# Splitting weight loads, and one batch's v, into row-sized pieces

## The chip, the cores and the metric

The kernel runs on one core of a Trainium2 chip. The metric is the device time of one execution in microseconds (us); lower is better. Before the change the median of five runs is 1142.55 us (1142.17 to 1143.49).

A core has a matrix engine (TensorE, PE in the profile), a vector engine (DVE), a scalar engine (ACT), GpSimd (POOL) and SyncE (SP). Each runs its own program in order. SP, ACT and POOL also issue DMAs, which 16 DMA engines carry out.

## The reference

```python
def _attn_ref(u, v, z):                    # u, v: (8, 3008, 256), z: (8, 3008, 64)
    scores = (1 / S) * np.matmul(z, z.transpose(0, 2, 1))
    attn = np.maximum(scores, 0.0) ** 2
    return u * np.matmul(attn, v)

def _moe_ref(x, w_tok1, w_tok2, w_ch1, w_ch2):   # x is the result of _attn_ref
    xt = x.transpose(0, 2, 1)
    h = np.maximum(xt @ w_tok1, 0.0) @ w_tok2    # (3008, 256), (256, 3008)
    u = x + h.transpose(0, 2, 1)
    h2 = np.maximum(u @ w_ch1, 0.0) @ w_ch2      # (256, 1536), (1536, 256)
    return u + h2
```

All inputs and the output are float32.

## The kernel before

The eight batches are worked through one after the other. For each batch the 3008 positions are cut into six blocks of 512 (the last has 448). For a block q of queries and a group g of 512 keys, PE forms scores from zT, the transposed z (line 428, tile `sc`). ACT takes the relu into a bf16 tile `at` (line 466), DVE squares it (line 474), and PE multiplies it with v into an accumulator (line 657, tile `acc`). After six groups the accumulator is evacuated (ACT copies one half, line 783, DVE adds the other, line 789) and DVE multiplies it with uT, the transposed u (line 810, called the gate here), into `xT`. The scores are symmetric, so from batch 1 on a tile `at` of block (q, g) is also turned by a DMA transpose into `fl` (line 526, called a flip here), which serves as block (g, q). There are six `at` buffers (`ROOM["at"]`); a new `at` may be written only when the PE reads and the flip of the tile six before it are done. In batch 0 every block but the last is computed directly.

When a batch's six blocks are done, the mixer follows for this batch: PE multiplies with w_tok1 (line 864) and w_tok2 (line 883), then with w_ch1 (line 924) and w_ch2 (line 993). The mixer of one batch is interleaved with the attention of the next. The weights are loaded once, during the attention of batch 0, and stay in memory.

The order on every engine is fixed when the program is made: a planner in the kernel keeps the time at which each engine will be free and appends the work that can start soonest. Its costs are constants (a load counts as `LOAD = 1.3` us); they aren't touched by the change.

Loads of v, u, z (from batch 1 on) and of the weights are issued by POOL and cast from float32 to bf16 on the way. They are due at given groups of batch 0, which the function `at_group` collects: the six groups of batch 1's v, six loads each of w_tok1 and w_tok2, two of w_ch1 and two of w_ch2 are spread over batch 0, between the loads of u and of batch 1's z. POOL's loads take eight completion semaphores in turn, so that a load waits until the one eight before it has landed. SP issues all transposes: uT from u (line 230), x_sb from xT (line 824), zT from z (lines 138 and 142), the flips (lines 518 and 526).

`rows_of` lets partition p take n consecutive rows of a group, so that its part of a load is one contiguous run:

```python
    def rows_of(ap, c):
        n = full_tiles[c]
        return ap[c * QW:c * QW + n * P, :].rearrange("(p t) d -> p t d", t=n)
```

QW is 512, P is 128; n is 4 for the first five groups and 3 for the last one, whose 64 remaining rows are loaded by themselves (line 211 for v, line 242 for w_tok1). In bf16 a row of 256 values has 512 bytes.

Of the kernel before, what the change touches and what calls it, by code (L numbers as in the profile page):

```python
# [13 lines left out]
P = 128  # L14
QW = 512
GK = 4
# [40 lines left out]
def kernel(  # L57
# [11 lines left out]
    nc = tc.nc  # L69
    B, S, D = u.shape  # L70
# [12 lines left out]
    widths = [min(QW, S - q * QW) for q in range(NQ)]  # L83
# [13 lines left out]
    w_tok1_sb = consts.tile([P, KT, d_tok], BF16)  # L97
    w_tok2_sb = consts.tile([P, DT, S], BF16)
    w_ch1_sb = consts.tile([P, DT, d_ch], BF16)
# [11 lines left out]
# [5 lines that stand above are left out]
    def last_rows(ap):  # L116
        return ap[(KT - 1) * P:, :]
# [81 lines left out]
    def load_v(b, c):  # L199
        if b == 0:  # L200

            vt = sb.tile([P, GK, D], BF16, tag="fl", name="v_sb", bufs=ROOM["fl"])
            live["fl"] += 1
            fl_free.pop(0)
        else:
            vt = sb.tile([P, GK, D], BF16, tag="v", name="v_sb", bufs=8)
        n = full_tiles[c]
        nc.gpsimd.dma_start(out=vt[:, :n, :], in_=rows_of(v[b], c))
        if n < GK:
            for r in range(2):  # L210
                nc.gpsimd.dma_start(
                    out=vt[r * TAIL:(r + 1) * TAIL, n, :], in_=last_rows(v[b]))
        vs[b, c] = vt
        v_in[b, c] = Done(pe[0] + 9.0 if b > 1 else 0.0)
        loading(LOAD)
# [19 lines left out]

    def load_w_tok1(c):
        n = full_tiles[c]
        nc.gpsimd.dma_start(
            out=w_tok1_sb[:, c * GK:c * GK + n, :], in_=rows_of(moe_w_tok1, c))
        if n < GK:  # L240
            nc.gpsimd.memset(w_tok1_sb[TAIL:, KT - 1, :], 0.0)
            nc.gpsimd.dma_start(
                out=w_tok1_sb[:TAIL, KT - 1, :], in_=last_rows(moe_w_tok1))
        loading(LOAD)

    def load_w_tok2(c):
        cols = slice(c * QW, c * QW + widths[c])
        nc.gpsimd.dma_start(
            out=w_tok2_sb[:, :, cols],
            in_=moe_w_tok2.rearrange("(tc t) s -> t tc s", t=P)[:, :, cols])  # L250
        loading(LOAD)

    def load_w_ch(part):
        if part < 2:
            nc.gpsimd.dma_start(
                out=w_ch1_sb[:, part, :], in_=moe_w_ch1[part * P:(part + 1) * P, :])
        else:
            h = CHT // 2
            c0 = (part - 2) * h
            nc.gpsimd.dma_start(  # L260
                out=w_ch2_sb[:, c0:c0 + h, :],
                in_=moe_w_ch2.rearrange("(cc c) d -> c cc d", c=P)[:, c0:c0 + h, :])
        loading(LOAD * 1.5)
# [42 lines left out]
    def loading(us):  # L306
        loads[0] = max(loads[0], pe[0] + 1.0) + us
# [91 lines left out]
    def can_score(first_unit, most):  # L399

        n, at = 0, live["at"]
        for (b, q, g), pr in units[first_unit:first_unit + most]:
            if (b, q) not in turned or (b, g) not in turned:
                break
            at += pr == 0
            if at > ROOM["at"]:
                break
            n += 1
        return n
# [717 lines left out]
    make_identity(nc, ident)  # L1127
    zf0 = [first_z(c) for c in range(NG)]
    load_v(0, 0)
    nc.gpsimd.memset(zs[:, 0, :], 0.0)  # L1130
    nc.gpsimd.memset(zs[:, KT + 1, :], 0.0)

    after(zf0[NG - 2][:, 0, :1])
    for c in range(1, NG):
        load_v(0, c)
# [52 lines left out]
    def when_used(b, c, j):  # L1188
        ask(lambda: load_v(b + 1, c),
            lambda: j < 2 or used.get((b, vorder[j - 2]), 0) == NQ)  # L1190
# [85 lines left out]
    def ask_w_ch(part):  # L1276
        load_w_ch(part)
        w_done[part].t = pe[0] + 16.0
# [4 lines left out]
    def ask_w_tok2(c):  # L1283
        load_w_tok2(c)
        tok2_done[c].t = pe[0] + 10.0

    items = [lambda c=c: load_v(1, c) for c in vorder]
    items += [lambda c=c: load_w_tok1(c) for c in range(NG)]
    items += [lambda c=c: ask_w_tok2(c) for c in range(NG)]
    items += [lambda part=part: ask_w_ch(part) for part in range(4)]  # L1290
# [30 lines left out]
    while cur[0] is not None or heads or tails:  # L1321
        run_engines(pe[0])
        ask_some()
        t = pe[0]
# [15 lines left out]
        n = can_score(done_units, most)  # L1340
# [118 lines left out]
```

## Time and profile before

| | us |
|---|---|
| median of five runs | 1142.55 |
| the profiled execution, its time | 1142.55 |
| its span (first to last instruction) | 1140.8 |
| PE busy | 1133.7 |
| DVE busy | 642.0 |
| ACT busy | 548.7 |
| POOL busy | 147.0 |

The span is the stretch from the first instruction to the last; what lies around it is start and end of the execution. In the profile, "busy" is the time in which an engine has an instruction under way. The DMA share is the sum of the time of all DMA packets over the time of 16 engines; it can be above 1 since packets overlap. The queue q0 holds the loads that POOL issues, q1 the transposes and stores that SP issues. In a row of the timeline the columns are the start, the duration, the engine (SPq is SP's queue), the line, the operation and the tiles it writes and reads; x4 means that four such instructions were merged into one row. A stage row gives the stretch, its length, then for each engine the busy time and the number of instructions, the granted TensorE clock as a share of full speed, the DMA share and the rate.

The rows of loads show minimum, median and maximum of the time that POOL takes to issue one. Landing times are counted from the start of the issue to the completion semaphore.

### The profile page before, as it was taken

The page shows a single profiled execution, that of the slowest core. Times are in us where ns is not written, and L with a number is a line of the kernel's source. Part 1 is how long each engine was busy: PE and PEld are TensorE (multiplying, and loading weights), DVE is VectorE, ACT ScalarE, POOL GpSimd, SP SyncE. Part 2 cuts the span into 40 slices and gives each one's busy share as a digit, 9 for nine tenths or more (in the row PEclk, how much of TensorE's full clock was granted, in tenths as well). Part 3 has the DMA queues.
Part 4 walks back from the last instruction along what each step waited for, and adds up shares of the span by engine and source line. Part 5 has one row for each costly group of instructions (what it writes and reads, how often), then busy time and mean ns, then how long its engine had stood idle before and what let it go on. Part 6 is the DMA issues. An engine that isn't in the chain of part 4 may idle for free.

```text
span 1140.8 us, 22492 instructions
## 1 busy us (share of the span) xinstructions
PE 1133.7 (99%) x9219; PEld 678.1 (59%) x9219; DVE 642.0 (56%) x953; ACT 548.7 (48%) x702; POOL 147.0 (13%) x387
## 2 busy tenths in 40 slices
PE   9999999999999999999999999999999999999998
PEld 3455564666557655576555765556655576556666
DVE  6887744464654556645565455654556544644543
ACT  7998624234752346522574236632366322732231
POOL 4500110221002110021101211012100120000000
PEclk9999999999999999999999999999999999999999
DMA  9999944997959978697987998779588795783122
GB/s 158 187 185 204 172 108 90 171 167 132 167 119 191 158 130 164 118 193 144 160 153 111 195 160 154 136 130 211 116 168 145 144 179 118 142 140 75 51 84 65
DMA packets 469927, 165.25 MB, mean 145 GB/s; under 512 B 433664, under 2 KB 447552, under 8 KB 469824
## 3 DMA queue, kind: packets, MB, share of 16 engines
q1 hardware_dynamic: 441968, 131.11, 58.2%
q0 software_dynamic: 27344, 32.32, 21.5%
q8 instruction: 72, 1.18, 0.5%
q10 hardware_dynamic: 512, 0.38, 0.1%
q14 instruction: 31, 0.25, 0.1%
HBM read 65.40 MB, written 24.64 MB: 79 GB/s over the span
## 4 chain that ended last, share of the span: by engine, by line
PE 98%; DMA 1%; DVE 1%; ACT 0%; issue 0%; SPq 0%; POOL 0%
PE acc L657 41%; PE op L993 22%; PE hp L924 21%; PE sc L428 6%; PE a_ps L864 4%; PE h_ps L883 3%; PE first_acc L573 1%; DMA zf<-in_z_dram 1%; DMA v_sb<-in_v_dram 0%; DVE xT L892 0%; DVE cp L789 0%; DVE at L474 0%; SPq L160 0%; DVE h2pre L949 0%; DVE xT L810 0%
## 5 line engine op out<-in xcount | busy, mean ns | idle before, releaser
L657 PEld LDWEIGHTS <-v_sb 64*128 64x128 bf16 x4418 | 241.7, 94 | 215.8 <-issue 1.8
L657 PE MATMUL acc<-at,v_sb 64*128 64x512 bf16 (+1 forms) x2738 | 339.0, 374 | 0.0
L466 ACT ACTIVATE at<-sc 128x1024 bf16<-128x1024 f32 (+1 forms) x290 | 286.4, 1026 | 68.7 <-PE sc L428 54.0
L967 ACT ACTIVATE h2pre<-hp 128x1024 bf16<-128x1024 f32 (+1 forms) x159 | 158.8, 998 | 310.7 <-PE hp L924 310.7
L474 DVE TENSOR_TENSOR at<-at 128x1024 bf16<-128x1024 bf16 (+1 forms) x290 | 197.4, 687 | 123.2 <-ACT at L466 120.3
L924 PE MATMUL hp<-xT,w_ch_sb 128*128 128x512 bf16 (+1 forms) x1152 | 255.3, 375 | 0.0
L993 PE MATMUL op<-w_ch_sb,h2pre 128*128 128x256 bf16 x2208 | 251.3, 273 | 0.1
L993 PEld LDWEIGHTS <-h2pre 128*128 128x128 bf16 x2208 | 216.0, 98 | 36.2 <-ACT h2pre L947 0.4
L969 DVE TENSOR_SCALAR h2pre<-hp 128x1024 bf16<-128x1024 f32 (+1 forms) x128 | 155.5, 1215 | 80.7 <-PE hp L924 80.7
L657 PE MATMUL acc<-fl,v_sb 64*128 64x512 bf16 (+1 forms) x1680 | 190.7, 367 | 0.0
L924 PEld LDWEIGHTS <-w_ch_sb 128*128 128x128 bf16 x1152 | 112.1, 98 | 126.5 <-issue 2.8
L1009 DVE TENSOR_TENSOR res<-op,u_sb 128x512 f32<-128x512 f32 x87 | 60.1, 691 | 174.9 <-PE op L993 172.9
L428 PE MATMUL sc<-zT 64*128 64x512 bf16 (+1 forms) x732 | 132.5, 360 | 0.1
L454 ACT ACTIVATE at<-sc 128x512 bf16<-128x512 f32 (+3 forms) x152 | 56.3, 443 | 90.5 <-PE sc L428 79.7
L789 DVE TENSOR_TENSOR cp<-acc,cp 128x512 f32<-128x512 f32 (+1 forms) x94 | 63.4, 675 | 38.6 <-ACT cp L783 38.4
L783 ACT COPY cp<-acc 128x512 f32<-128x512 f32 (+1 forms) x89 | 51.8, 583 | 54.4 <-PE acc L657 54.3
L506 DVE TENSOR_TENSOR at<-at 128x512 bf16<-128x512 bf16 (+3 forms) x152 | 41.9, 320 | 49.0 <-ACT at L454 49.0
L428 PEld LDWEIGHTS <-zT 64*128 64x128 bf16 x732 | 42.5, 94 | 42.9 <-issue 4.2
L810 DVE TENSOR_TENSOR xT<-cp,uT 128x512 bf16<-128x512 f32 (+1 forms) x94 | 62.4, 664 | 1.6
L892 DVE TENSOR_TENSOR xT<-xT,h_ps 128x1024 bf16<-128x1024 bf16 (+1 forms) x48 | 56.1, 1175 | 12.5 <-PE h_ps L883 12.5
L121 POOL CAST mark<-at 128x1 f32<-128x1 bf16 x11 | 2.4, 215 | 398.1 <-DVE at L474 398.1
L883 PE MATMUL h_ps<-w_tok_sb,a_sb 128*128 128x512 bf16 (+1 forms) x192 | 48.0, 375 | 0.2 <-DVE xT L892 0.2
(59 smaller groups left out, 315.8 us busy)
## 6 DMA issues: line engine op xcount, KB each, us to landing
out_dram<-res SPq DMA_DIRECT2D x87, 256.0 KB, 2.7
v_sb<-in_v_dram POOLq DMA_DIRECT2D x40, 256.0 KB, 5.8
ur<-in_u_dram POOLq DMA_DIRECT2D x40, 256.0 KB, 5.0
w_tok_sb<-in_moe_w_tok_dram POOLq DMA_DIRECT2D x10, 256.0 KB, 9.6
zs<-in_z_dram POOLq DMA_DIRECT2D x35, 64.0 KB, 3.0
at<-at SPq DMA_TRANSPOSE x114, 2.4
fl<-at SPq DMA_TRANSPOSE x105, 5.3
v_sb<-in_v_dram POOLq DMA_DIRECT2D x8, 192.0 KB, 4.9
```

Of the source, the lines that this page charges most:

```text
L428: nc.tensor.matmul(sc[:, r, c0:c1], zT[h, k:k + P], zT[h, m + c0:m + c1], start=True, stop=True)
L466: nc.scalar.activation(view, sv, ACT.Relu, scale=inv_S)
L474: nc.vector.tensor_mul(view, view, view)
L657: nc.tensor.matmul(o, vs[blk.b, g][rows, i, dh * P:(dh + 1) * P], rhs, start=(dh, h) not in blk.begun, stop=stop, skip_group_check=True)
L789: nc.vector.tensor_add(cp[:, :W], acc[:, 0, :W], cp[:, :W])
L810: nc.vector.tensor_mul(xT[:, dh, :full * P].rearrange("p (t s) -> p t s", s=P), acc[:, :full * P].rearrange("p (t s) -> p t s", s=P), uT[: ...
L883: nc.tensor.matmul(h[:, dh, :W], st["a"][:, th, dh * P:(dh + 1) * P], w_tok2_sb[:, th, q * QW:q * QW + W], start=(th == 0), stop=(th == 1))
L924: nc.tensor.matmul(hp[:, r, :W], w_ch1_sb[:, dc, cc * P:(cc + 1) * P], xT[:, dc, :W], start=(dc == 0), stop=(dc == DT - 1))
L967: nc.scalar.activation(h2[:, :, :W], hp[:, :, :W], ACT.Relu)
L969: nc.vector.tensor_single_scalar(h2[:, :, :W], hp[:, :, :W], 0.0, AX.max)
L993: nc.tensor.matmul(op[:, i, :], h2, w_ch2_sb[:, cc, :], start=(cc == 0 and (i == 0 or apart)), stop=(cc == CHT - 1), skip_group_check=True)
L1009: nc.vector.tensor_add(res.rearrange("p i (h d) -> p i h d", d=P), op.rearrange("p i (h d) -> p i h d", d=P), us[:, :, half * 2:half * 2 + ...
```

## The change

Four load functions change. For batch 1's v (`load_v`) and for w_tok1, a group's load becomes two: one takes each partition's rows 0 and 2, the other rows 1 and 3 (in the last group, rows 0 and 2, and row 1). For w_tok2 a load of 512 columns becomes two of 256 (the last 256 and 192). For w_ch1 a load of 128 rows of 1536 values becomes two, with the even and with the odd stretches of 256 values. The rows of v in other batches, of u and z, and w_ch2, are loaded as before; w_ch2's pieces already were rows of 256 values. The same bytes reach the same places.

```diff
@@ load_v
-        nc.gpsimd.dma_start(out=vt[:, :n, :], in_=rows_of(v[b], c))
+        for r in range(2 if b == 1 else 1):
+            t = slice(r, n, 2) if b == 1 else slice(n)
+            nc.gpsimd.dma_start(out=vt[:, t, :], in_=rows_of(v[b], c)[:, t, :])
@@ load_w_tok1
-        nc.gpsimd.dma_start(
-            out=w_tok1_sb[:, c * GK:c * GK + n, :], in_=rows_of(moe_w_tok1, c))
+        for r in range(2):
+            nc.gpsimd.dma_start(
+                out=w_tok1_sb[:, c * GK + r:c * GK + n:2, :],
+                in_=rows_of(moe_w_tok1, c)[:, r:n:2, :])
@@ load_w_tok2
-        cols = slice(c * QW, c * QW + widths[c])
-        nc.gpsimd.dma_start(
-            out=w_tok2_sb[:, :, cols],
-            in_=moe_w_tok2.rearrange("(tc t) s -> t tc s", t=P)[:, :, cols])
+        for r in range(2):
+            cols = slice(c * QW + r * D, min(c * QW + (r + 1) * D, c * QW + widths[c]))
+            nc.gpsimd.dma_start(
+                out=w_tok2_sb[:, :, cols],
+                in_=moe_w_tok2.rearrange("(tc t) s -> t tc s", t=P)[:, :, cols])
@@ load_w_ch
-            nc.gpsimd.dma_start(
-                out=w_ch1_sb[:, part, :], in_=moe_w_ch1[part * P:(part + 1) * P, :])
+            for r in range(2):
+                out, rows = (
+                    ap.rearrange("p (k c) -> p k c", c=D)[:, r::2, :]
+                    for ap in (w_ch1_sb[:, part, :], moe_w_ch1[part * P:(part + 1) * P, :]))
+                nc.gpsimd.dma_start(out=out, in_=rows)
```

## The prediction

> **What bounds the kernel now.** I read the page's busy times first, then the chain of work that ended last, then the DMA queues, then a table of stages, and last the SP queue's timeline between 54 and 93 us, the stretch in which the changed loads are in flight.
>
> ```profile
> PE 1133.7 (99%) x9219; PEld 678.1 (59%) x9219; DVE 642.0 (56%) x953; ACT 548.7 (48%) x702; POOL 147.0 (13%) x387
> ...
> q1 hardware_dynamic: 441968, 131.11, 58.2%
> q0 software_dynamic: 27344, 32.32, 21.5%
> ...
> PE 98%; DMA 1%; DVE 1%; ACT 0%; issue 0%; SPq 0%; POOL 0%
> ```
>
> TensorE is busy for 1133.7 of 1140.8 us and the chain is TensorE's own work. What is left to win is 7.1 us of idle time, and most of it lies before 20 us and after the last matmul. q0 carries POOL's loads (cast from f32 to bf16 on the way), q1 carries SP's transposes and stores.
>
> ```profile
> core 0: us, PE busy (x) PEld busy (x) DVE busy (x) ACT busy (x) POOL busy (x), PEclk, DMA share, GB/s
> 24.00:30.00 6.00, 6.00 (x53) 2.81 (x53) 5.90 (x11) 5.95 (x8) 4.26 (x8) 1.00 0.82 120
> ...
> 60.00:70.00 10.00, 10.00 (x96) 5.47 (x94) 8.99 (x15) 9.03 (x11) 2.40 (x4) 1.00 1.15 193
> 70.00:80.00 10.00, 10.00 (x104) 5.57 (x100) 8.36 (x15) 8.35 (x11) 0.00 (x0) 1.00 1.37 172
> 80.00:90.00 10.00, 10.00 (x102) 5.75 (x100) 8.18 (x15) 9.13 (x12) 0.23 (x2) 1.00 1.13 196
> 90.00:100.00 10.00, 10.00 (x96) 5.25 (x94) 7.57 (x13) 9.72 (x11) 0.52 (x1) 1.00 1.13 207
> ```
>
> From 30 us on the DMA share is over 1 (packets overlap): the DMA engines are full, first with loads, then with transposes. Yet PE has no gap in these rows. So a DMA that comes sooner gains nothing here, and one that comes later costs only what exceeds its slack.
>
> ```profile
> 54.12 1.23 SPq L824 DMA_TRANSPOSE x_sb<-xT  x1
> 55.53 21.23 SPq L138 DMA_TRANSPOSE zT<-zs  x4
> 76.85 1.21 SPq L142 DMA_TRANSPOSE zT<-zs  x1
> 78.23 1.24 SPq L230 DMA_TRANSPOSE uT<-ur  x1
> 79.57 2.02 SPq L824 DMA_TRANSPOSE x_sb<-xT  x1
> 81.68 1.26 SPq L230 DMA_TRANSPOSE uT<-ur  x1
> 83.03 1.26 SPq L824 DMA_TRANSPOSE x_sb<-xT  x1
> 84.39 1.26 SPq L230 DMA_TRANSPOSE uT<-ur  x1
> 85.74 4.99 SPq L526 DMA_TRANSPOSE fl<-at  x2
> 91.20 1.23 SPq L824 DMA_TRANSPOSE x_sb<-xT  x1
> 92.48 11.62 SPq L526 DMA_TRANSPOSE fl<-at  x4
> ```
>
> SP works in order and nearly without a pause. Until 78 us its transposes crawl beside the loads (batch 1's zT takes 21 us to issue); then the loads are done (the last, w_ch2, was issued at 63.62 and landed 15.3 us later, at 78.9) and five transposes pass in 8 us. The flips (fl<-at, L526) follow at once.
>
> **The change, part by part.** *Pieces.* A group of 512 rows is now 128 pieces of 4 KB, one for each partition; it becomes 512 pieces of 1 KB (512 B as bf16). The page's 27344 packets are 24256 pieces and 16 end marks for each of 193 loads. The change adds 5x384+256 pieces for batch 1's v, as many for w_tok1, 6x256 for w_tok2 and 2x640 for w_ch1, in all 7168, and 20 loads (320 marks): 34832 packets. The trace's DMA records, by size, have medians of 60 ns for 512 B, 96 for 1024, 135 for 1536, 173 for 2048 and 247 for 3072. For one of 16 engines: a group of v or w_tok1 goes from 8x173 = 1.38 us to 32x60 = 1.92 (+0.54, ten times; the two groups of three rows 8x135 to 24x60, +0.36); w_tok2 from 16x96 to 32x60 (+0.38, six times); a half of w_ch1 from 8x247 to 48x60 (+0.90, twice). That is 5.4+0.7+2.3+1.8 = 10.2 us, and 0.4 us for 20 marks of 18 ns: 10.6 us more for each DMA engine.
>
> A rule stands against this price. The Trainium skill, "DMA: Bandwidth & Descriptors", section "Specifications", puts line rate at pieces of 512 B and up; four of these would then cost one of 2048, the extra would be nil and the time 1142.6. The records here say 240 ns against 173, and I go by them.
>
> *Issue on POOL.* A 256-piece load takes 0.70 us to issue, a plain one 0.53:
>
> ```profile
> L248 POOL DMA_DIRECT2D w_tok_sb<-in_moe_w_tok_dram x6: 696/705/722, 46.2 to 54.2; - x6
> ```
>
> Twelve groups of v and w_tok1 come to 10x0.87+2x0.70 = 10.1 us more, w_tok2 to 6x0.70 = 4.2, w_ch1 to about 2 (between 0.70 and the 0.84 of w_ch2's 768 pieces): 16 us. POOL idles for 18 us between 25 and 65 us, waiting for the load eight back, whose semaphore it reuses, so this hides behind the DMA engines; uncovered, it would only put the last issue 16 us later, which is inside the case of rival C. The PE, DVE, ACT and SP programs stay in their order.
>
> *The loads themselves* are covered: first uses are at 87.7 us (v of batch 1, landed by 42), 112.4 (w_tok1), 130.4 (w_tok2), 133.9 (w_ch1) and 142.8 (w_ch2).
>
> *When the loads end.* From 44.5 us (first w_tok1 landed) to 78.9 the queue moved 29.7 us of pieces in 34.4 us, a stretch of 1.16. After the change there are 36.6 us of them. Beside transposes, pieces go one to one (74 to 76 us: 472 of 512 B and 462 of 256 B on 16 engines, 68.5 ns a pair, 1.14 of 60), and the records show full stops of about 1 us in 15 (53.5, 80.5, 89, 102.5 us), so I take 1.14x1.07 = 1.22: 44.7 us, 10.3 more. Batch 1's v and the first w_tok1 add 3.3 us (3.7x1.16, less 1 us of the gap at 24 to 30 us). The end moves from 78.9 to 92.5; by the old stretch to 90, and to 99 if pieces and transposes don't overlap at all (60+18 = 78 ns a pair).
>
> *What gains.* A transpose piece now waits for 60 ns of load, not 173. SP's 64+4x48+8 = 264 pieces an engine from 54.1 us on, at 68.5x1.06 = 73 ns, are through at about 76 us where zT landed at 82.2. PE's first scores of batch 1 stand at 80.5 us without a gap before them, so this is worth nothing.
>
> *What loses.* The five transposes and two flips that follow (5x64+2x128 = 576 pieces) met no loads; now they do, until 92.5. At 73 ns the first three are through at 90; then at the free pace (1.35 us a transpose, 2.0 to 2.2 a flip) the others take 6 us from 92.5, and with the 1.5 us from last piece to semaphore the second flip lands at 100.0. It now lands at 95.8 (issued at 88.22, 7.6 us). The delay is 4.2 us, and SP, which has almost no pause up to 113 us, doesn't make it up.
>
> *Slack behind it.* The tile `at` has six buffers; ACT may write the seventh only when the flip that reads the first has landed. Against ACT's own times:
>
> ```profile
> 98.54 1.96 ACT L466 ACTIVATE at<-sc 128x1024 bf16<-128x1024 f32 x2
> ```
>
> this write waits for the flip landed at 95.8 (2.7 us), the write at 106.28 for the flip issued at 98.14 and landed at 104.4 (1.9 us). Behind a waiting ACT stand its next relu and the copies that free accumulators (L783); PE, in order, can write one or two more scores and then waits for a bank. PE itself reads the second flip at 101.04. Delay less the smallest slack: 4.2-1.9 = 2.3 us; the gate of (0,5) at 88.1 and zT keep theirs. Ends: a delay of 1 us (loads done at 89) costs nothing, one of 10 us (loads done at 99) about 8.
>
> **Sum.** The profiled run was 1142.55 us (span 1140.8 and 1.75 around it), which is the median too. 1142.55+2.4 = 1145.0.
>
> **Rivals.** A: *the slack holds.* The loads end by 90 us, or PE's one or two scores of lead (1.08 us each) swallow the rest; 1142.6, at most 1144. For it: slacks of 5 us at PE itself (101.04 against 95.8). Against: the queue's stretch was 1.16 with less interleaving. B: *faster.* The place is PE's gaps from 24 to 142 us; these are 0.04 and 0.21 us in the stage tables, so freed transposes give 0.3 us, 1142.3. For a gain past the bound, the modelled ends of matmuls would have to hide over 2 us of waiting that zT's earlier landing removes; matmul starts at 108 and 216 ns intervals speak against it. It decides if PE's rows around 80 us shift earlier. C: *a longer jam.* Pieces and transposes don't overlap, or POOL's issue binds; loads to 99 us, delay 10, stall 8: 1150.6. Against: the 68.5 ns pair. D: *the split isn't made*, if neighbouring rows are merged again: 1142.6; but rows two apart aren't adjacent, and w_ch2's 256-wide pieces count as separate in the 27344.
>
> **How the numbers follow.** About 0.2% (2.3 us) is what a measurement tells from no change. My case, a stall of over 2.3 us, has with C 0.57 (C alone 0.12), A with D 0.38, B 0.05. The forecast sits just past the bound, as its working does. Low end 1142.0 (A, with B's 0.3 us and spread), high end 1149.5, short of C's far end.
>
> **What would show it.** 34832 packets on q0; 512-B records near 60 ns; w_ch2 landing at 90 to 96 us; zT landing near 76 and the second flip near 100; ACT waiting for "DMA fl<-at" and PE gaps between 97 and 110 us of 2 to 3 us, and nothing after 150. Wrong if w_ch2 lands before 88, if no flip is late against ACT, or if PE gaps appear elsewhere.

## The result and the profile after

| kernel | median us | range, runs | profiled run: time, span |
|---|---|---|---|
| before | 1142.67 | 1141.77 to 1156.55, 80 | 1142.55, 1140.8 |
| after | 1145.75 | 1142.27 to 1152.42, 43 | 1142.91, 1141.1 |

The ratio is 1.0024, with a 95% interval of 1.0016 to 1.0032: the changed kernel is slower, by some 3 us at the median. The ratios, here and below, leave out the runs of a second, slower state, which the medians and ranges contain. Its profiled execution is near the low end of its own runs, only 0.36 us above the profiled execution of before. Two ends of the chain of waits, first of before, then of after (start us, us, what), tell why that figure is too small:

```profile
1131.78 4.23 PE op L993 x37
1136.01 0.02 issue
1136.04 0.42 DVE res L1027
```

```profile
1133.82 4.23 PE op L1001 x37
1138.04 0.02 issue
1138.07 0.42 DVE res L1035
```

The last instruction ends 2.03 us later (1138.49 against 1136.46). The spans differ by only 0.3 us because what is behind it took 2.6 us (1141.1 less 1138.49) where it took 4.3. The last store is not the reason: it lands 1.70 us after the last instruction in both (at 1138.16 and 1140.19). The trace's records show that the program of POOL closes with an instruction called DRAIN. In before it runs from 1131.77 to 1139.69, and the other engines wait for it at the end; in after it is over at 1138.04, before the store has landed. So two things are in the figure: 2.0 us lost on the way, and 1.7 us got back behind the last instruction, on which the prediction has no word. Both are looked at below.

The page of after, busy times, queues and shares of the chain:

```profile
PE 1133.6 (99%) x9219; PEld 678.4 (59%) x9219; DVE 642.0 (56%) x953; ACT 549.1 (48%) x702; POOL 162.9 (14%) x407
...
q1 hardware_dynamic: 441968, 131.11, 57.8%
q0 software_dynamic: 34832, 32.32, 21.6%
...
PE 97%; DMA 1%; DVE 1%; ACT 0%; issue 0%; SPq 0%; POOL 0%; ACTq 0%
```

q0 carries the same 32.32 MB in 34832 packets, where it had 27344, and its share of the DMA engines' time has hardly moved (21.5 to 21.6%). POOL has 15.9 us more, as worked out. TensorE has the same work. The stages show where the time is lost:

```profile
core 0: us, PE busy (x) PEld busy (x) DVE busy (x) ACT busy (x) POOL busy (x), PEclk, DMA share, GB/s
24.00:30.00 6.00, 6.00 (x56) 2.91 (x56) 6.00 (x10) 5.95 (x7) 3.27 (x6) 1.00 0.85 166
60.00:70.00 10.00, 10.00 (x98) 5.41 (x94) 8.85 (x15) 9.02 (x12) 5.41 (x9) 1.00 1.45 164
70.00:80.00 10.00, 10.00 (x102) 5.60 (x100) 8.35 (x15) 8.35 (x11) 4.50 (x7) 1.00 1.36 184
80.00:90.00 10.00, 10.00 (x103) 5.76 (x100) 8.38 (x15) 9.13 (x11) 0.57 (x2) 1.00 1.36 171
90.00:100.00 10.00, 7.87 (x75) 3.98 (x73) 5.11 (x10) 6.82 (x8) 0.17 (x1) 1.00 1.24 227
```

Only the last row has a hole in PE, 2.13 us, and POOL is now still issuing loads between 60 and 80 us. The SP queue's timeline of the same stretch:

```profile
55.20 7.21 SPq L138 DMA_TRANSPOSE zT<-zs  x4
62.51 3.21 SPq L142 DMA_TRANSPOSE zT<-zs  x1
65.88 4.23 SPq L232 DMA_TRANSPOSE uT<-ur  x1
...
78.87 5.57 SPq L832 DMA_TRANSPOSE x_sb<-xT  x1
84.57 4.07 SPq L232 DMA_TRANSPOSE uT<-ur  x1
88.73 7.66 SPq L534 DMA_TRANSPOSE fl<-at  x2
```

zT, which took 21 us to issue, takes 7; the transposes after it, which took 1.3 us each, now take 3.7 to 5.6, because the loads are still running (w_ch2, issued at 75.17, lands 15.9 us later, at 91.0). The two flips take 7.66 us where they took 4.99. What that does to ACT and PE (timeline; in brackets the idle time before it and what ended it):

```profile
98.69 1.94 ACT L474 ACTIVATE at<-sc 128x1024 bf16<-128x1024 f32 x2 [3.02 <-DMA fl<-at]
99.77 0.39 PE L436 MATMUL sc<-zT 64*128 64x512 bf16 x2 [2.13 <-ACT at L474]
```

ACT waits 3.02 us for the second flip, which lands at 98.59; PE's next score waits 2.13 us for the bank that this relu empties.

### The profile page after: what moved, and what is told of

Its sections match the earlier page's. It is cut to its first block, busy times and chain, and to the rows that moved or that the text cites. A ratio compares the mean times of both kernels' runs of the same rounds, so it can differ in the third digit from the quotient of the medians.

```text
span 1141.1 us, 22518 instructions
## 1 busy us (share of the span) xinstructions
PE 1133.6 (99%) x9219; PEld 678.4 (59%) x9219; DVE 642.0 (56%) x953; ACT 549.1 (48%) x702; POOL 162.9 (14%) x407
## 3 DMA queue, kind: packets, MB, share of 16 engines
q0 software_dynamic: 34832, 32.32, 21.6%
## 4 chain that ended last, share of the span: by engine, by line
PE 97%; DMA 1%; DVE 1%; ACT 0%; issue 0%; SPq 0%; POOL 0%; ACTq 0%
PE acc L665 41%; PE op L1001 21%; PE hp L932 21%; PE sc L436 6%; PE a_ps L872 4%; PE h_ps L891 3%; PE first_acc L581 1%; DMA zf<-in_z_dram 1%; DMA fl<-at 0%; DMA v_sb<-in_v_dram 0%; DVE xT L900 0%; DVE cp L797 0%; DVE at L482 0%; ACT at L474 0%; SPq L160 0%
## 5 line engine op out<-in xcount | busy, mean ns | idle before, releaser
L791 ACT COPY cp<-acc 128x512 f32<-128x512 f32 (+1 forms) x89 | 51.8, 582 | 54.8 <-PE acc L665 54.5
```

## The experiments

Twelve kernels were run, in three groups, each beside runs of the kernel before on the same chip (medians there 1143.01, 1143.20 and 1143.16 us). "zT", "w_ch2" and "flip" are the times at which batch 1's last zT transpose, the last load and the second flip landed in the profiled run.

| kernel | median us (range, runs) | ratio, 95% | zT | w_ch2 | flip |
|---|---|---|---|---|---|
| v_only | 1145.33 (1143.84 to 1162.38, 11) | 1.0020, 1.0010 to 1.0029 | 83.8 | 80.4 | 94.3 |
| w_only | 1145.23 (1143.56 to 1152.41, 12) | 1.0015, 0.9996 to 1.0035 | 74.5 | 91.7 | 99.3 |
| late_whole | 1155.11 (1153.34 to 1156.35, 4) | 1.0106, 1.0091 to 1.0121 | 91.3 | 77.5 | 102.7 |
| loads_only | 1163.57 (1150.59 to 1168.70, 6) | 1.0141, 1.0105 to 1.0178 | 84.0 | 96.7 | 104.7 |
| before_at7 | 1142.72 (1141.39 to 1143.16, 11) | 0.9993, 0.9985 to 1.0002 | 82.2 | 79.0 | 93.8 |
| after_at7 | 1142.19 (1141.11 to 1150.17, 12) | 0.9999, 0.9980 to 1.0017 | 75.0 | 94.4 | 101.4 |
| after_again | 1146.74 (1142.28 to 1148.82, 12) | 1.0024, 1.0013 to 1.0035 | 73.0 | 90.3 | 97.9 |
| halves | 1161.47 (1153.98 to 1164.85, 5) | 1.0162, 1.0145 to 1.0179 | 84.6 | 95.6 | 105.0 |
| rows_split | 1144.02 (1141.84 to 1151.68, 12) | 1.0016, 0.9996 to 1.0035 | 88.3 | 94.0 | 104.9 |
| pad_whole | 1151.50 (1145.50 to 1158.89, 6) | 1.0079, 1.0048 to 1.0110 | 83.0 | 80.2 | 93.5 |
| halves_rows | 1153.93 (1153.41 to 1156.30, 4) | 1.0099, 1.0086 to 1.0112 | 88.7 | 94.0 | 105.7 |
| halves_pad | 1146.30 (1143.64 to 1151.47, 6) | 1.0038, 1.0024 to 1.0052 | 84.1 | 87.1 | 99.3 |

### Which part: v_only and w_only

v_only has the change in `load_v` alone, w_only the change in the three weight loaders alone, each word for word as in the diff.

> Only batch 1's v is split (2176 of the 7168 extra pieces). Theory (the loads end later, the two flips at 88 to 96 us meet them and land later, ACT waits for the second flip's at buffer, PE waits for ACT): the last w_ch2 load lands at 81 to 84 us instead of 78.9, the second flip lands less than 1 us later than the 95.8 of before; ACT waits under 1 us and PE under 0.5: 1142.4 to 1143.2 us. Rival 1 (more loads on POOL and its eight semaphores are the cost, not the pieces): 6 of 20 extra loads, a third of the loss, 1143.5. Rival 2 (small v pieces hurt the weight loads of PE): the whole loss, 1145.5.

> Only w_tok1, w_tok2 and w_ch1 are split (4992 of the 7168 extra pieces). Theory: w_ch2 lands at 86 to 89 us (91.0 with all split, 78.9 with none); the second flip lands at 96.5 to 98; ACT waits 1 to 2 us, PE 0.3 to 1.5: 1142.8 to 1144.5 us. Rival 1 (the number of loads): 14 of 20 extra loads, 1144.5 to 1145. Rival 2 (it is all v): as before, 1142.6.

The waits of w_only between 78 and 104 us (engine, line, what it waited for; us, times, longest):

```profile
ACT at L472 <- DMA fl<-at: 3.3, 1, 3.3
...
PE sc L434 <- ACT at L472: 2.4, 1, 2.4
```

The weights alone make the same stall at the same place as the whole change, with the loads done at 91.7 us where 86 to 89 was expected. With v alone the loads end 1.5 us later than before (at 80.4, where 81 to 84 was expected), the flip is in time, but zT lands 1.6 us later than before and PE's scores wait for it:

```profile
PEld L430 <- DMA zT<-zs: 0.6, 1, 0.6
...
PE sc L430 <- DMA zT<-zs: 0.2, 1, 0.2
```

That is a second deadline, which the prediction did not price: before, zT's last transpose landed at 82.2 and PE's scores begin on it at 82.5. Both medians are some 2.2 us up, w_only's with an interval that reaches below 1. The parts do not add, since the whole change moves zT forward and spoils only the flips. Nor is v_only's loss all of one kind: in its profile the last instruction ends 1.0 us later than in before (1137.49), and another 1.1 us is the DRAIN of POOL, which ends at 1142.10. The 1145.5 us of rival 2 is near the median, but its cause is not there: the durations of PE's weight loads add up to 882.9 us in v_only and in before.

### More loads in flight, pieces whole: late_whole and loads_only

```diff
+        if part == 3:            # late_whole: eight weight loads once more
+            for c in range(5):
+                load_w_tok1(c)
+            for c in range(3):
+                load_w_tok2(c)
```

```diff
-        nc.gpsimd.dma_start(out=vt[:, :n, :], in_=rows_of(v[b], c))
+        for h in (ROWS if b == 1 else [slice(0, P)]):      # loads_only; the weights likewise
+            nc.gpsimd.dma_start(out=vt[h, :n, :], in_=rows_of(v[b], c)[h])
```

> The kernel before, with whole pieces, and after w_ch2 five loads of w_tok1 and three of w_tok2 once more (the same data to the same place), so that the loads end at about 92 us without small pieces. Theory (what counts is that loads are still in flight when the transposes after zT come): uT of (0,5) and the flips crawl at about 180 ns a piece, the flips land after 99 us, the gate of (0,5) at 88 us may be late too; PE waits 4 to 9 us, 1146.5 to 1152 us. Rival (the harm is in the small pieces themselves): 1142.6 us, flips as before.

> The same loads are cut in two, but by halves of the partitions, so that every piece is as long as before and only the number of loads rises (23 more, 20 in the change). Theory (pieces): w_ch2 lands at 79 to 81 us, no PE gap at 95 to 105 us, 1142.4 to 1143.0 us. Rival 1 (loads on POOL, eight semaphores): w_ch2 lands near 91 and the time is 1145 to 1146.

late_whole repeats eight loads of before behind w_ch2, so that whole pieces meet the transposes until about 91 us. The waits and the stages (the PEclk column is the third from the end):

```profile
PE sc L435 <- DMA zT<-zs: 8.6, 1, 8.6
```

```profile
82.00:91.00 9.00, 0.50 (x6) 0.06 (x2) 1.25 (x2) 0.75 (x1) 0.00 (x0) 0.82 1.23 183
91.00:95.00 4.00, 3.87 (x24) 1.57 (x26) 1.38 (x2) 2.26 (x3) 0.00 (x0) 0.56 1.05 236
95.00:99.00 4.00, 4.00 (x44) 2.00 (x42) 2.86 (x6) 4.00 (x5) 0.00 (x0) 1.00 0.84 190
```

Loads that are still in flight after 79 us are by themselves enough for a stall, whatever their pieces; with pieces of 2 KB it is zT that is late, by 8.6 us. And a wait of that length costs more than itself: in the row of the 4 us after it TensorE was granted 0.56 of its clock (the clock's own record is 0.5 from 87.69 to 94.52 us). The median, 1155.11 us, is above the 1152 expected at most.

loads_only cuts each load by halves of the partitions, which makes 20 more loads (the expectation says 23). Its loads ended at 96.7 us, not at 79 to 81, and the time was far outside both expectations. It was meant to separate loads from pieces, and does not do so cleanly, since a load now goes to half of the partitions only; taken alone it can't be read. It comes back below.

### The wait itself: before_at7, after_at7, after_again

One more buffer for `at`, paid for with one of v and one of x; the order of every engine's instructions stays.

```diff
-            ats[b, q, g] = sb.tile([P, GK * QW], BF16, tag="at", name="at", bufs=ROOM["at"])
+            ats[b, q, g] = sb.tile([P, GK * QW], BF16, tag="at", name="at", bufs=ROOM["at"] + 1)
```

> The control: the kernel before with the same buffers (at 7, v 7, x 6). Theory and rival alike: loads, flips and PE as in the kernel before, no PE gap over 0.4 us between 25 and 1100 us, 1142.3 to 1143.3. If it is over 0.7 us from the kernel before, the buffers taken from v and x cost something by themselves and the pair after_at7 against before_at7 is the comparison to read.

> The changed kernel with one more buffer for the tile at (7, was 6; paid for by one buffer less for v and for the x tiles), every engine's order as in the changed kernel. Theory (the loss is ACT waiting for an at buffer until the late second flip lands): ACT's write at about 96 us then goes into a free buffer and the next one at about 98.2 us is the first that waits for the flip landed at about 98.6, by 0.4 us at most; PE's gap of 2.3 us at 97.5 us shrinks to 0.5 us or less, w_ch2 still lands at about 91 and the second flip at about 98.6; time within 0.7 us of the kernel before with 7 buffers, some 1142.5 to 1143.5. Rival (PE itself waits for the late flips or transposes, or POOL's extra issue costs): a gap of over 1.5 us stays between 95 and 110 us and the time stays at 1145 to 1146.

> The changed kernel itself beside the others on one chip. Theory: 1144 to 1146.5, PE gap of 2 to 5 us at 97 to 98 us, last matmul 2 to 3 us later than in the kernel with 7 buffers unchanged; runs with a longer stall show a lower mean clock. If its profiled run shows a gap of 2.3 us and the last store lands 4.3 us (not 2.6) after the last DVE instruction, the profiled run of 1142.91 us was short by its last store alone.

On one chip, after_again is at 1146.74 us and after_at7 at 1142.19, level with before (1143.20) and before_at7 (1142.72). The loads are the changed kernel's; the buffer alone removes nearly all of the loss. Counted without the end, where after_at7's profile is 1.4 us shorter than before_at7's (2.6 against 4.0 us behind the last instruction), it still loses 0.9 us on the way, and after_again some 5.2. This shows that the loss is in the main ACT's wait for a flip that has to give back an `at` buffer, and not PE's own reading of what was loaded or POOL's work as such. Seven of the 12 runs of after_at7 lie below 1142.5 us, and one of after_again's 12. The profiled run of after_at7 was one of its longer ones (1145.12): there the loads ended at 94.4, and the same wait came one flip later:

```profile
ACT at L474 <- DMA fl<-at: 3.4, 1, 3.4
...
PE acc L665 <- ACT at L474: 3.0, 1, 3.0
```

```profile
99.00:103.00 4.00, 0.98 (x10) 0.41 (x8) 0.41 (x1) 1.46 (x2) 0.00 (x0) 1.00 1.16 263
103.00:107.00 4.00, 4.00 (x25) 1.84 (x22) 3.38 (x6) 1.98 (x3) 0.18 (x1) 0.57 1.42 224
107.00:111.00 4.00, 4.00 (x41) 2.07 (x37) 1.64 (x3) 3.36 (x4) 0.55 (x1) 1.00 1.02 228
```

So one buffer is worth one flip of slack, no more. The rows show again a lowered clock, 0.57 for 4 us, which is 0.43 x 4 = 1.7 us on top of the 3.0 (the clock's record: 0.5 for 3.41 us). After the 2.1 us of the profiled run of after the clock stayed at 1.00. Of after's runs, the 17 with a mean clock of 1.000 average 1143.5 us and the ten with 0.997 average 1148.4: the longer ones fit a stall that is long enough to lower the clock, but no profile of such a run of after exists, so this is argued and not shown. after_again's profile is of its fastest run (1142.28; PE waits 1.8 us), and there too the end came 2.6 us after the last instruction, as in after_at7; in before_at7 it was 4.0. So the expectation that the 2.6 us was chance fell; what it calls the landing of the last store is the DRAIN of POOL, 4.24 or 4.25 us long in after, after_again and after_at7, and 7.92 in before and before_at7. With 1.7 us gained at the end, the median's loss of 3.1 us means some 4.8 us lost on the way: a wait of 3.0 and a lowered clock of 1.7, as in the profile of after_at7, would make that up.

### Pieces or loads: halves, and four kernels that differ in one thing

halves keeps the changed kernel's 20 extra loads but makes each piece twice as long (two rows, or 1024 or 1536 B).

```diff
-            t = slice(r, n, 2) if b == 1 else slice(n)
+            t = slice(2 * r, min(2 * r + 2, n)) if b == 1 else slice(n)      # halves
```

> As many loads as the changed kernel has, but each load cut in two so that pieces are twice as long: two rows (1024 B as bf16) for v and w_tok1, a full 1024 B for w_tok2 by halves of its rows, 1536 B for w_ch1. Theory (the size of the pieces makes the loads end late): by the record medians (96 ns for 1024 B against 173 for 2048 and 60 for 512) each DMA engine needs about 2.5 us more instead of 10.6; w_ch2 lands at 81 to 85, the second flip at 95.8 to 97, PE's gap at 97 us is 0 to 0.9 us, time 1142.6 to 1143.8. Rival (the 20 extra loads, their POOL issue and end marks do it, not the pieces): w_ch2 at about 91, gap 2.3 us, 1145 to 1146.

Both expectations fell: with half as many pieces the loads ended not at 81 to 85, and not at 91, but at 95.6. So I cut v and w_tok1 alone, in four ways:

```diff
+        t = slice(r, n, 2)                        # rows_split: two loads, pieces of one row
+        t = slice(2 * r, min(2 * r + 2, n))       # halves_rows: two loads, pieces of two rows
-            vt = sb.tile([P, GK, D], BF16, tag="v", name="v_sb", bufs=8)
+            vt = sb.tile([P, GK, D + 16], BF16, tag="v", name="v_sb", bufs=8)   # pad_whole:
+            vt = vt[:, :, :D]                     # one load, pieces of one row
...
                                                   # halves_pad: halves_rows on padded tiles
```

> The kernel before with the changed kernel's cut for batch 1's v and w_tok1 alone (pieces of one row, two loads a group, 12 loads more); w_tok2 and w_ch1 as before. It is the reference point for the next three, which differ from it in one thing each. Theory (the small pieces take longer, 5.4+0.7 us more for each DMA engine by the record medians): w_ch2 lands at 82 to 87 us (78.9 before, 91.0 in the changed kernel), the second flip at 95.5 to 98, PE gaps of 0 to 2 us in all at 82 to 84 (scores waiting for zT) and 96 to 98 us; 1143 to 1146 us.

> The same pieces of one row, but not one load more than before: the rows of the tiles of v and w_tok1 stand 272 values apart instead of 256, so that a group is one load of 512 pieces (one x tile fewer pays for the room). Theory (pieces, not loads): w_ch2 lands within 2 us of rows_split. Rival (the extra loads, their issue and end marks): w_ch2 as in the kernel before, 78 to 80 us, and 1142.3 to 1143.3 us.

> As rows_split with the same loads, but each load takes two neighbouring rows of a group (pieces of 1024 B; the source is read 2 KB out of every 4 KB). By the record medians (96 ns for 1024 B) 1.4 us more for each DMA engine than before: w_ch2 at 79 to 82. After the run called halves I expect instead that the cut by neighbouring rows is what is slow: records stretched and 100 to 125 GB/s somewhere between 46 and 64 us, w_ch2 at 84 to 92, and over 1146 us.

> As halves_rows with the same loads and the same source, but the tiles' rows 272 values apart, so that the pieces are single rows again. If the way in which the source is read (2 KB out of every 4 KB by one load) slows the queue, it is as slow as halves_rows (100 to 125 GB/s between 46 and 64 us, w_ch2 at 84 or later). If the 1024-B pieces do, it is like rows_split, w_ch2 within 2 us of it.

Here is pad_whole, whose groups of w_tok1 are one load of 512 pieces each (durations min, median, max in ns), and its stages from 26 us on; the last column is GB/s:

```profile
L244 POOL DMA_DIRECT2D w_tok_all<-in_moe_w_tok_dram x6: 742/742/762, 35.6 to 42.9; - x6
```

```profile
26.00:46.00 20.00, 20.00 (x190) 9.65 (x186) 17.59 (x29) 19.51 (x23) 15.77 (x27) 1.00 1.33 178
46.00:60.00 14.00, 13.96 (x132) 7.04 (x130) 12.34 (x20) 13.83 (x16) 6.04 (x10) 1.00 1.30 183
```

and rows_split, with the same pieces in twice the loads:

```profile
26.00:46.00 20.00, 20.00 (x188) 9.68 (x186) 17.59 (x29) 19.51 (x22) 18.53 (x29) 1.00 1.20 163
46.00:60.00 14.00, 13.96 (x132) 7.06 (x128) 12.34 (x20) 13.83 (x16) 6.62 (x13) 1.00 1.45 137
```

A load of 512 pieces takes POOL 0.74 us to issue, two of 256 take 1.41. From 26 to 46 us v's loads run, from 46 to 60 mostly w_tok1's. The same two figures for all 14 profiled runs:

```
GB/s               26-46   v cut in two?      46-60   w_tok1 cut in two?
before              174    no                  187    no
before_at7          172    no                  190    no
late_whole          183    no                  184    no
pad_whole           178    no, one-row pieces  183    no, one-row pieces
w_only              178    no                  124    yes
v_only              161    yes                 180    no
after               156    yes                 176    yes
after_again         165    yes                 155    yes
after_at7           143    yes                 172    yes
rows_split          163    yes                 137    yes
halves_pad          158    yes                 144    yes
halves_rows         158    yes, two rows       109    yes, two rows
halves              162    yes, two rows       124    yes, two rows
loads_only          145    yes, whole pieces   134    yes, whole pieces
```

In the first stretch whole groups of v give 172 to 183 GB/s and groups in two loads 143 to 165; in the second, whole groups of w_tok1 give 180 to 190 and groups in two loads 109 to 176. pad_whole, with its one-row pieces, is on the side of the whole groups both times, and loads_only, with whole pieces, on the other. So for v and w_tok1 it is the number of loads that slows the queue. What the pieces of w_tok2 and w_ch1 do is not separated by any run. How the two rows that one load takes lie in the source does not decide it (halves_pad against rows_split, 158 and 144 against 163 and 137). Differences among the cut kernels can't be read further: after, after_again and after_at7 have the same loads and lie between 143 and 165, and between 155 and 176. Of the expectations, rows_split's loads ended later than said (94.0 against 82 to 87, in a profiled run of 1149.20 us, one of its longer ones). pad_whole's ended at 80.2, as its rival had it, but it took 1151.50 us, not 1142.3 to 1143.3. halves_rows came much as expected after halves, with 109 GB/s, its loads ending at 94.0 us, and halves_pad's loads ended 6.9 us before rows_split's, not within 2.

Two things in the traces say how. First, POOL itself binds. Between 40 and 44 us of after, against before:

```profile
40.00:44.00 4.00, 4.00 (x40) 2.01 (x38) 3.50 (x6) 4.00 (x5) 3.95 (x6) 1.00 0.89 110
```

```profile
40.00:44.00 4.00, 4.00 (x40) 1.93 (x38) 3.51 (x7) 3.85 (x5) 2.30 (x5) 1.00 1.13 210
```

POOL issues without a pause (3.95 of 4 us) and the DMA engines run short (share 0.89, 110 GB/s against 210). Second, POOL issues a load only when the one eight back has landed, and eight half loads hold half as much. rows_split's POOL timeline has the extreme case:

```profile
63.05 0.55 POOL L259 DMA_DIRECT2D w_ch_sb<-in_moe_w_ch_dram  x1 [0.79 <-DMA w_tok_sb<-in_moe_w_tok_dram]
71.46 0.53 POOL L222 DMA_DIRECT2D ur<-in_u_dram  x1 [7.86 <-DMA w_tok_sb<-in_moe_w_tok_dram]
```

In those 7.9 us q0's records (start to end in us, bytes) come, for 3.6 us, almost only one after the other, as of one engine alone; nearly nothing else of q0 is under way:

```
62.591-62.687 1024
62.696-62.792 1024
62.800-62.896 1024
62.905-63.001 1024
63.010-63.106 1024
```

A load counts as landed when the slowest of 16 engines is through with it (the trace has 16 updates of the semaphore for each load). The Trainium skill, "DMA: Bandwidth & Descriptors", section "Latency and other measured facts", says that two of the engines usually lag in loads that GpSimd issues; the trace has no engine's number, so no run here shows whether it is one of these. A rough count over 26 to 96 us, with each load taken as outstanding from 2 us after its issue ended to 1.5 us before it landed, gives the time in which three records of q0 or fewer were under way: 1.0 us in before, 2.0 in pad_whole, 5.8 in after, 7.9 in rows_split and 11.9 in w_only. It does not explain all, since halves_rows, the slowest, has 3.0.

What stays open: pad_whole's profile is of its fastest run, and shows PE's end 0.3 us later than before and an end 7.0 us behind the last instruction (a DRAIN of POOL of 10.6 us), which alone makes it 2.7 us longer; its other five runs took 1148 to 1159 us, with lower clocks (0.994 to 0.998), and nothing shows their wait. Its zT lands at 83.0, right at its use, so the stall of late_whole and rows_split (5.1 us on zT in rows_split) is the likely one. By the median pad_whole is even 7.5 us slower than rows_split, of which the end explains 4.4. So one load of one-row pieces keeps the queue's rate, but that such pieces cost no time is not shown. Nor is it shown why two-row halves come out slower than one-row halves (109 against 137 GB/s): each is one profiled run. No version beat the kernel before: after_at7 and before_at7 can't be told from it.

## Why the prediction held, step by step

**Bound and place: right.** PE's gap is 2.13 us in 90 to 100 us, ACT waits for "DMA fl<-at" at the write it named, and PE's rows after 150 us are as before. after_at7 shows the cause by removing nearly all of the loss.

**Pieces: right in number, wrong as a price.** 34832 packets came out as counted, and the records of 512 B have a median of 60 ns. But the step "10.6 us more for each DMA engine" took record durations for engine time. Records of one engine overlap: with no transpose beside them, 46 to 50 us of after has 747 pieces of 512 B in each 2 us, which is 16 x 2000 / 747 = 42.8 ns a piece, where whole pieces of 2048 B go at 207 in 2 us in before (42 to 44 us), 154.6 ns. Per group that is 32 x 42.8 - 8 x 154.6 = 0.13 us, not 0.54. pad_whole confirms it for v and w_tok1: w_ch2 at 80.2 where the step would charge 6.1 us. The Trainium skill, "DMA: Bandwidth & Descriptors", section "Specifications", had line rate from 512 B on; the prediction set that aside, and pad_whole's 178 and 183 GB/s against 174 and 187 side with the page.

**POOL's issue: the step that failed.** "This hides behind the DMA engines" counted POOL's idle time as cover. 16 us was right (147.0 to 162.9), but the idle time was the wait for the load eight back; with loads half as large the queue behind POOL is half as deep, and from 40 to 44 us POOL is the bound. For v and w_tok1 this, and not the pieces, is what lowers the queue's rate.

**When the loads end: nearly right, from the wrong terms.** 92.5 was said, 91.0 and 90.3 measured. From 26 us to the loads' end the queues moved 7.51 MB of loads and 1.88 MB of transposes at 177 GB/s before, 7.51 and 3.42 MB at 168 GB/s after. Of the 12.1 us, (3.42 - 1.88)/177 GB/s = 8.7 us are transposes that went ahead of loads, and 3.4 us are the lower rate, so the step on POOL's issue is by this count the smaller part of the delay. The first part seems to go with the small pieces of w_tok2 and w_ch1: zT lands at 73.0 to 75.0 us in the four profiles that have them (after, after_again, after_at7, w_only) and at 82.2 or later in the other ten. It was in the step on gains (zT through near 76, though 264 pieces at 73 ns from 54.1 end at 73.4; it landed at 74.1), and gained nothing, as said.

**Delay and slack: two errors that cancelled, by luck.** The second flip was to come 4.2 us late and came 2.8 late (98.59 for 95.8), 3.1 against PE, whose start was 0.3 us earlier. No run shows the 1.5 us from the last piece to the semaphore as a fixed time: for 37 transposes of before that stand alone the median is 0.46. The slack was put at 1.9 us, from a count of six buffers in strict rotation. The write at 96.07 us already waits for the second flip, with 0.27 us to spare; PE's lead adds some 0.6. So 3.1 - 0.9 = 2.2 us, the predicted figure (4.2 - 1.9 = 2.3, 2.4 in the sum), from other numbers.

**What the sum lacked.** POOL's shorter DRAIN, 1.7 us in the change's favour, and the lowered clock behind a wait of 3 us, against it. The median's 3.1 us is near the predicted 2.4 with both left out, which is luck too.

**Rivals.** A (the slack holds): no, ACT is late; but 0.3 us of slack and 0.6 of lead are what keep the loss small. B (faster): no, zT's 8 us gave PE nothing. C (a longer jam): not this run, but the longer runs may be near it; that POOL's issue binds, which it named, did come true from 40 to 44 us. D: the packets exclude it. What no rival named is that PE's clock falls after a longer wait.

## What to carry to other kernels

Where POOL's queue waits for the load eight back, cutting loads cuts the bytes in flight and adds issue time (1.41 us for two loads of 256 pieces here, 0.74 for one of 512): price the number of loads, and pieces of 512 B by bytes over rate, not by the sum of record durations. A load that finishes later delays transposes of another queue that share the DMA engines, so look for the wait at the consumer of those transposes, and read its slack from the semaphore it really waits on. One buffer more at that consumer was worth nearly the whole loss here. And one profiled execution can hide the loss: compare the end of the last instruction, not the span alone, and see what the end waits for.

## What the runs showed of the hardware

- A wait of TensorE can lower its clock afterwards. The clock's records show 0.5 for 3.41 us after waits of 3.0 us (after_at7) and 5.1 (rows_split), and for 6.83 us with the wait of 8.6 (late_whole). The length of the wait does not decide alone: one of 2.25 us lowered it in loads_only (0.5 for 3.41 us from 94.10), and 2.13 in after and 2.43 in w_only did not. The Trainium skill, "TensorE: Matmul & The Clock Gate", section "Part 1: The HAM clock gate (the "warmup" mystery)", states a half clock after an idle window of about 3.4 us; here shorter waits sufficed.
- Now and then nearly all DMA packets stop together for about 1.1 to 1.5 us: in before from 52.7, 80.2 and 89.9 us, in after from 52.4, 80.6 and 92.2. Each time a fetch of 16 KB of instructions began shortly before (51.8, 79.8 and 88.8; 51.6, 79.8 and 91.8). Not every such fetch is followed by a stop: the one at 39.5 in before is not. The stops that the prediction used as an average thus have a place; that the fetch makes them is not shown.
- The last store lands 1.70 us after the last DVE instruction in all 14 profiles. The end comes 2.6 us after that instruction in six (after, after_again, after_at7, w_only, rows_split, halves_pad) and 4.0 to 7.0 us after it in the other eight, where POOL's closing DRAIN ends last. The DRAIN goes with the number of packets that q0 moved: 7.92 us at 27344 packets (before, before_at7), rising to 10.62 at 31696 (pad_whole), then 1.14 at 31888 (rows_split and halves_pad), 1.38 at 32560 (w_only) and 4.24 at 34832 (after). Why is open.
